# A Fourier filter with a gated convolution: other figures in the planner, seven subtractions on GpSimd, and a new order

## The chip, the cores and the metric

The kernel runs on one core of one Trainium2 chip. The time is device microseconds of that core, from the start of the program to its end; "before" is the median of three runs. The profile shows one further execution. Engines are named as the profile names them: PE (TensorE, matmuls; PEld its weight loads), DVE (VectorE), ACT (ScalarE), POOL (GpSimd), SP (SyncE, which issues most DMAs).

## The reference

Input x is 8 x 3200 x 256 in float32. A real Fourier transform runs along the 3200 positions, a complex 256 x 256 matrix mixes the channels, a bias is added, real and imaginary part are shrunk softly by 0.01, and the inverse transform goes back. The result passes a causal convolution of five taps per channel, a sigmoid, and a gate:

```
X = rfft(x, axis=1)
Yr = Xr @ w_r - Xi @ w_i + b_r ;  Yi = Xr @ w_i + Xi @ w_r + b_i
Y  = soft(Yr, 0.01) + 1j * soft(Yi, 0.01)        # sign(v) * max(|v| - lam, 0)
y  = irfft(Y, n=3200, axis=1)
gate = sigmoid(sum_k conv_w[k] * y[position - 4 + k])
out  = (gate * (y @ w_val)) @ w_out
```

## The kernel before

**Tiling.** The 3200 positions are 64 x 50. Each of the 8 batches goes through these stages; the names are those of the profile's rows (line numbers of the kernel before; behind line 350 the changed kernel's are one or two higher).

- P1 (L583; L549 for batch 0): the transform of length 50, in 8 parts of 400 KB of x. ACT copies the product to `s`, SP stores it to `a_dram`.
- 13 spectrum steps u, the last of half size. s2 (L634) multiplies `a`, read back from `a_dram`, by the twiddled matrix `f_sb`. ACT and DVE split the result into a high part (rounded) and a low part (the remainder), and do the same for the sum of its real and imaginary part (DVE L691, L692, L696). The complex mixing is done in three real products: the sum product (L709, into `k_bank`) and the mix (L704, into `y_ps`); for the half step it is L667 and L668. DVE adds the bias (L715; L670 for the half step) and the sum (L718), ACT and DVE shrink softly (L722, L724), and every second step the inverse product S1I (L747; L739 for the half step) goes through ACT to `z_dram`.
- 8 blocks of positions: `zl` is read back from `z_dram`, the inverse transform of length 50 (L803) gives `y_p`, ACT copies it to `y_sb`; behind the last block of a batch DVE copies the convolution's border (L816, L822).
- Gated convolution: ACT does the first tap (L857), DVE the other four (L860) on two blocks at a time, ACT the sigmoid (L871). y is split (ACT L360 high, DVE L362 remainder, tile `y_hl`), the v product (L835) follows, DVE multiplies the gate in (L902), the result is split in the same way (tile `gated`), the o product (L835) follows, ACT copies it to `o` (L926), SP stores it. For the last nine blocks (block 7 of batch 6 and all of batch 7, the list LATE_VAL) the v product works on unsplit y (L831, tile `w_late`, which POOL makes from the split weights, L937).

At the start matrix pieces are turned on PE (L469) for the inverse, and PE is kept busy with warm-up products on zeros (L951).

**What sets the order.** The program is first collected as pieces (function `add`: engine, duration, what it uses, what it sets, buffers). `Plan.order` then runs a list schedule over them with its own model: durations per engine (`dve`, `act`), DMA rates (RATE, PIPE), a fetch of the instructions of PE in packets (AHEAD, PACKET, TRIGGER, FETCH, QUEUE). Whenever several pieces could begin, the smallest due time `at` wins; due times are the step's place plus an offset from the table `O`. The engines run their queues in that order, so a changed figure can move any instruction. `WARM[2]` is the number of warm-up products ahead of the first s2. `split` makes a pair of high part and remainder. Pools set what can overlap: `ps_2` has two buffers, which P1, S1I, the positions, v and o all take in turn.

The seven blocks that the change's new flag picks are blocks 0 to 6 of batch 6: `LATE` lists the blocks of batches 6 and 7, and these seven are not in LATE_VAL.

## Time and profile before

| what | value |
|---|---|
| median of 3 runs | 879.93 us (878.89 to 881.42) |
| profiled execution | 881.59 us |
| its span, first to last instruction | 879.8 us |
| mean granted clock of PE | 0.994 |
| busy: PE, PEld, DVE, ACT, POOL | 857.8, 745.5, 759.1, 604.9, 3.8 us |
| bytes read from HBM and written to it | 82.05 and 79.69 MB |

A busy engine is one with an instruction in flight. Matmuls overlap, so the durations of their rows add up to more than the time they take; the distance from the start of one row to the next is what a product costs. An f32 matmul shows as two records, an fp32r one as one.

### The profile page before, as it was taken

Reading aid. Unit: us, or ns where it says so; the run is one execution under the profiler, and the core shown is the slowest. Engines: PE = TensorE matmul, PEld = TensorE weight load, DVE = VectorE, ACT = ScalarE, POOL = GpSimd, SP = SyncE. Lnnn points to the kernel's source line nnn. Section 1 sums busy time; section 2 is a strip of 40 time slices with the busy share of each in tenths; the row PEclk is TensorE's granted clock in tenths of the full one; section 3 lists DMA queues with packets and bytes.
Section 4 is the critical chain, followed back from the end, with each engine's and each line's share of the span. In section 5 each row is a group of like instructions: output and inputs, shape, how many; then the busy total and the mean of one; then the engine's idle time right before and its main releaser. Section 6 shows DMA issues by size and latency. Waiting matters only on the chain.

```text
span 879.8 us, 24544 instructions
## 1 busy us (share of the span) xinstructions
PE 857.8 (97%) x10400; PEld 745.5 (85%) x10400; DVE 759.1 (86%) x1143; ACT 604.9 (69%) x928; POOL 3.8 (0%) x11
## 2 busy tenths in 40 slices
PE   7999999999999999999999999999999999998997
PEld 3778788878999898898899889898899999998775
DVE  2346888999989996999879997899969999899796
ACT  2456666977677766877667776877658775875664
POOL 0000000000000000000000000000100000000000
PEclk9999999999999999999999999999999999999999
DMA  6878886786554476565855576646746353423522
GB/s 212 253 244 253 240 269 197 265 251 199 165 184 146 148 218 212 177 185 172 272 168 171 175 237 205 218 122 208 244 133 202 104 171 94 142 103 110 186 76 94
DMA packets 105289, 163.34 MB, mean 186 GB/s; under 512 B 9690, under 2 KB 78172, under 8 KB 105180
## 3 DMA queue, kind: packets, MB, share of 16 engines
q1 hardware_dynamic: 103764, 158.43, 58.1%
q10 hardware_dynamic: 1416, 3.34, 1.2%
q8 instruction: 82, 1.34, 0.6%
q14 instruction: 27, 0.22, 0.1%
HBM read 82.05 MB, written 79.69 MB: 184 GB/s over the span
## 4 chain that ended last, share of the span: by engine, by line
PE 78%; DVE 15%; DMA 3%; ACT 2%; issue 1%; SPq 0%; ACTq 0%; DVEq 0%
PE y_ps L704 14%; PE o_ps L835 12%; PE v_ps L835 11%; PE s L634 9%; PE z_ps L747 8%; PE k_bank L709 7%; PE y_p L803 6%; DVE acc L860 6%; PE p L583 5%; DMA x<-in_x 2%; PE warm L951 1%; DVE acc L902 1%; PE v_ps L831 1%; DMA f_sb<-in_f 1%; DVE gated L362 1%
## 5 line engine op out<-in xcount | busy, mean ns | idle before, releaser
L860 DVE SCALAR_TENSOR_TENSOR acc<-y_sb,cw_sb,acc 128x800 f32<-128x800 f32 (+1 forms) x264 | 258.7, 1017 | 11.4 <-ACT acc L857 11.2
L704 PE MATMUL y_ps<-w_sb,xs 128*128 128x256 f32 x1152 | 157.7, 286 | 0.7 <-DVE yb L718 0.7
L835 PE MATMUL o_ps<-gated,wo_sb 128*128 128x400 f32 x756 | 153.5, 352 | 0.0
L704 PEld LDWEIGHTS y_ps<-w_sb,xs 128*128 128x128 f32 x1152 | 144.3, 190 | 8.6 <-issue 3.9
L835 PEld LDWEIGHTS o_ps<-gated,wo_sb 128*128 128x128 f32 x756 | 135.6, 189 | 3.4 <-issue 1.0
L835 PE MATMUL v_ps<-y_hl,wv_sb 128*128 128x400 f32 x660 | 130.6, 346 | 1.1 <-ACT y_sb L810 1.1
L634 PEld LDWEIGHTS s<-f_sb,a 128*128 128x128 f32 x800 | 100.3, 191 | 24.9 <-issue 19.0
L835 PEld LDWEIGHTS v_ps<-y_hl,wv_sb 128*128 128x128 f32 x660 | 118.7, 188 | 2.1 <-ACT y_sb L810 1.3
L634 PE MATMUL s<-f_sb,a 128*128 128x128 f32 x800 | 111.9, 280 | 1.3 <-DVE xs L692 1.2
L747 PE MATMUL z_ps<-tp,g_sb 64*64 64x256 f32 x1536 | 93.7, 380 | 0.0
L688 ACT CAST xs<-s 128x512 fp32r<-128x512 f32 x96 | 56.2, 586 | 43.0 <-PE y_ps L704 28.1
L709 PE MATMUL k_bank<-w_sb,xs 128*128 128x256 f32 x576 | 85.3, 283 | 0.4 <-DVE yb L715 0.4
L722 ACT ACTIVATE tp<-yb,nlam 128x512 f32<-128x512 f32 (+1 forms) x104 | 73.6, 708 | 16.5 <-DVE yb L718 9.0
L718 DVE TENSOR_TENSOR yb<-y_ps,yb 128x512 f32<-128x512 f32 x96 | 65.4, 681 | 19.9 <-PE y_ps L704 19.7
L747 PEld LDWEIGHTS z_ps<-tp,g_sb 64*64 64x64 f32 x1536 | 57.1, 133 | 27.1 <-issue 5.8
L360 ACT CAST gated<-acc 128x800 fp32r<-128x800 f32 x63 | 54.2, 861 | 37.1 <-DVE acc L902 33.5
L709 PEld LDWEIGHTS k_bank<-w_sb,xs 128*128 128x128 f32 x576 | 74.8, 188 | 5.1 <-issue 1.1
L926 ACT COPY o<-o_ps 128x800 f32<-128x800 f32 x63 | 51.9, 823 | 38.0 <-PE o_ps L835 37.8
L803 PEld LDWEIGHTS y_p<-g_sb,zl 50*64 50x64 f32 x4096 | 66.1, 135 | 13.9 <-issue 5.1
L902 DVE TENSOR_TENSOR acc<-v_ps,acc 128x800 f32<-128x800 f32 x64 | 62.9, 983 | 16.9 <-PE v_ps L835 14.1
L724 DVE SCALAR_TENSOR_TENSOR tp<-yb,tp 128x512 f32<-128x512 f32 (+1 forms) x104 | 68.8, 661 | 7.7 <-ACT tp L722 7.4
L803 PE MATMUL y_p<-g_sb,zl 50*64 50x50 f32 x4096 | 71.8, 220 | 3.4 <-issue 2.2
(80 smaller groups left out, 1028.4 us busy)
## 6 DMA issues: line engine op xcount, KB each, us to landing
zl<-z_dram SPq DMA_DIRECT2D x128, 200.0 KB
out<-o SPq DMA_DIRECT2D x63, 400.0 KB
a_dram<-s SPq DMA_DIRECT2D x120, 208.0 KB
a<-a_dram SPq DMA_DIRECT2D x96, 256.0 KB
z_dram<-z_t SPq DMA_DIRECT2D x48, 512.0 KB
x<-in_x SPq DMA_DIRECT2D x120, 200.0 KB
...
```

Of the source, the lines that this page charges most:

```text
L634: nc.tensor.matmul(spec()[:, c, :, i, :], tl[ka][:, i0 + i, c * P:(c + 1) * P], f2_of(i), start=True, stop=True)
L688: nc.scalar.copy(out=tl[kx][:, 0:512], in_=tl[k2].rearrange("p a b -> p (a b)"))
L704: nc.tensor.matmul(p[:, 1 - r, :], xm(hx, c, r), w_sb[:, m, hw, c, :], start=k == 0, stop=k == 5)
L709: nc.tensor.matmul(p, sm(hx, c), w_sb[:, 0, hw, c, :], start=k == 0, stop=k == 5)
L718: add(at + 0.2, "DVE", dve(2 * D), lambda: nc.vector.tensor_tensor(out=yb(), in0=tl[ky], in1=yb(), op=ALU.add), [ky + (0,)], [kb + (0,)])
L722: nc.scalar.activation(out=buffer(kt, "tp", [P, 2, D])[:, 0:n], in_=tl[kb][:, 0:n], func=AF.Relu, bias=nlam)
L724: add(at + 0.2, "DVE", dve(n * D), lambda: nc.vector.scalar_tensor_tensor(out=tl[kt][:, 0:n], in0=tl[kb][:, 0:n], scalar=LAM, in1=tl[kt][: ...
L747: nc.tensor.matmul(p[e * HP:(e + 1) * HP, i, j * D:(j + 1) * D], g[i * HP:(i + 1) * HP, r, e * HP:(e + 1) * HP], tl[kts[j]][i * HP:(i + 1) ...
L803: nc.tensor.matmul(pv[h][e * HP:(e + 1) * HP, c, m, :], zt[half(h), m, c * P + e * HP:c * P + (e + 1) * HP], g2_sb[half(h), :], start=True ...
L835: nc.tensor.matmul(p[:, e, 0:TB], w[:, hw, c, e * P:(e + 1) * P], src(hy, c), start=n == 0, stop=n == 5)
L860: nc.vector.scalar_tensor_tensor(out=acc(c), in0=y_of(c, j), scalar=cw_sb[:, c, j:j + 1], in1=acc(c), op0=ALU.mult, op1=ALU.add)
L902: add(at + own("gate", b), "DVE", dve(2 * TB), lambda: nc.vector.tensor_tensor(out=gate(), in0=hn(tl[kv][:, :, 0:TB]), in1=gate(), op=ALU. ...
```

## The change

Figures of the planner:

```diff
-PIPE = {10: 235, 13: 300, 16: 324}
+PIPE = {10: 212, 13: 300, 16: 324}
-AHEAD, PACKET, TRIGGER, FETCH, QUEUE = 449, 256, 130, 5200, 0.6
+AHEAD, PACKET, TRIGGER, FETCH, QUEUE = 449, 256, 130, 7000, 0.6
-O = {'stay': -42.085,
+O = {'stay': 0.402,
...
-     's2': -2.447,
+     's2': -1.427,
...
-     'mix_sum': -0.971,
+     'mix_sum': -0.252,
...
-WARM = 4, 1, 19
+WARM = 4, 1, 10
+POOL_LOW = 2.7
```

PIPE and FETCH are the planner's own model: loads over ten DMA engines are taken as slower, the fetch of PE's instruction packets as longer. The table `O` is new in all its 35 entries. The remainder of y may go to GpSimd, and the last warm-up products are fewer and wider:

```diff
-    def split(at, n, key, src, high, low, uses=(), new=None, first=None):
+    def split(at, n, key, src, high, low, uses=(), new=None, first=None, pool=False):
...
-        add(at + 0.001, "DVE", dve(n), lambda: nc.vector.tensor_tensor(out=low(), in0=src(), in1=f32(high()), op=ALU.subtract),
+        eng, busy = ("POOL", POOL_LOW * n) if pool else ("DVE", dve(n))
+        add(at + 0.001, eng, busy, lambda: (nc.gpsimd if pool else nc.vector).tensor_tensor(out=low(), in0=src(), in1=f32(high()), op=ALU.subtract),
             [*uses, hl[0]], [hl[1]])
...
-                         lambda: buffer(ky, "y_hl", [P, 2, 2, TB], F32R)), ("w", "w_val", "high"), ("w", "w_val", "low")]
+                         lambda: buffer(ky, "y_hl", [P, 2, 2, TB], F32R), pool=bk in LATE), ("w", "w_val", "high"), ("w", "w_val", "low")]
...
-    def warm(n):
+    def warm(n, w=2 * P):
...
-            nc.tensor.matmul(pw.rearrange("p a b -> p (a b)")[:, 0:2 * P], tl[ki][:, 0:P], tl[ki][:, 0:2 * P], start=True, stop=True)
+            nc.tensor.matmul(pw.rearrange("p a b -> p (a b)")[:, 0:w], tl[ki][:, 0:P], tl[ki][:, 0:w], start=True, stop=True)
...
-        add(-22, "PE", 430, lambda: warm(1), [ki + (0,), ("turn", "p1", 7)], [kw + ("end", i)], ins=4)
+        add(-22, "PE", 860, lambda: warm(1, 4 * P), [ki + (0,), ("turn", "p1", 7)], [kw + ("end", i)], ins=4)
```

What it moves is shown at three places. First PE at the start, from the first sum product on (`k_bank<-w_sb` is the sum product, `k_bank<-eye_sb` a turning product, `s` is s2, `y_ps` the mix, `p` is P1). Before:

```order
L709 MATMUL k_bank<-w_sb,xs 128x256 x6
L583 MATMUL p_321<-x,f_sb 64x512 x4
L634 MATMUL s_308<-f_sb,a 128x2x64 x2
L583 MATMUL p_336<-x,f_sb 64x512 x4
L704 MATMUL y_ps<-w_sb,xs 128x256 x12
L583 MATMUL p_365<-x,f_sb 64x512 x4
L709 MATMUL k_bank<-w_sb,xs 128x256 x6
L634 MATMUL s_389<-f_sb,a 128x2x64 x2
L469 MATMUL k_bank<-eye_sb,f_sb 128x128 x2
L634 MATMUL s_389<-f_sb,a 128x2x64 x2
L469 MATMUL k_bank<-eye_sb,f_sb 128x128 x4
L704 MATMUL y_ps<-w_sb,xs 128x256 x12
```

Now:

```order
L711 MATMUL k_bank<-w_sb,xs 128x256 x6
L585 MATMUL p_312<-x,f_sb 64x512 x4
L706 MATMUL y_ps<-w_sb,xs 128x256 x12
L585 MATMUL p_341<-x,f_sb 64x512 x4
L585 MATMUL p_349<-x,f_sb 64x512 x4
L636 MATMUL s_299<-f_sb,a 128x2x64 x2
L711 MATMUL k_bank<-w_sb,xs 128x256 x6
L706 MATMUL y_ps<-w_sb,xs 128x256 x12
L471 MATMUL k_bank<-eye_sb,f_sb 128x128 x4
L636 MATMUL s_401<-f_sb,a 128x2x64 x2
L471 MATMUL k_bank<-eye_sb,f_sb 128x128 x4
L585 MATMUL p_415<-x,f_sb 64x512 x4
```

The second mix stands ahead of the turning products, which stood ahead of it, and the half s2 that stood ahead of the first of them now stands behind two.

Second, PE behind the half mix of the last batch, up to the position products (`y_p`) of that batch (`z_ps` is S1I, the single one of 128x256 the last). Before:

```order
L835 MATMUL o_ps<-gated,wo_sb 128x400 x12
L835 MATMUL v_ps<-y_hl,wv_sb 128x400 x12
L747 MATMUL z_ps<-tp,g_sb 64x256 x16
L739 MATMUL z_ps<-tp,g_sb 128x256
L835 MATMUL o_ps<-gated,wo_sb 128x400 x12
L835 MATMUL v_ps<-y_hl,wv_sb 128x400 x12
L835 MATMUL o_ps<-gated,wo_sb 128x400 x12
L835 MATMUL v_ps<-y_hl,wv_sb 128x400 x12
L831 MATMUL v_ps<-y_sb,w_late 128x400 x4
L803 MATMUL y_p<-g_sb,zl 64x50 x96
```

Now:

```order
L837 MATMUL v_ps<-y_hl,wv_sb 128x400 x12
L837 MATMUL o_ps<-gated,wo_sb 128x400 x12
L749 MATMUL z_ps<-tp,g_sb 64x256 x16
L837 MATMUL v_ps<-y_hl,wv_sb 128x400 x12
L837 MATMUL o_ps<-gated,wo_sb 128x400 x12
L741 MATMUL z_ps<-tp,g_sb 128x256
L837 MATMUL v_ps<-y_hl,wv_sb 128x400 x12
L837 MATMUL o_ps<-gated,wo_sb 128x400 x12
L837 MATMUL v_ps<-y_hl,wv_sb 128x400 x12
L833 MATMUL v_ps<-y_sb,w_late 128x400 x4
L837 MATMUL o_ps<-gated,wo_sb 128x400 x12
L805 MATMUL y_p<-g_sb,zl 64x50 x64
```

Four products of twelve matmuls stand ahead of the last S1I, and two did; one v product more stands behind the half mix than before.

Third, DVE over the same stretch, from the bias addition of the half mix on, with the numbers of the names, which rise in the order of issue over all engines (`acc<-y_sb` are taps, `acc<-v_ps` the gate products, `gated` and `y_hl` remainders). Before:

```order
L670 TENSOR_TENSOR yb_10340<-y_ps_10314,bias_sb_75 128x256
L362 TENSOR_TENSOR gated_10338<-acc_9963,gated_10338 128x800
L724 SCALAR_TENSOR_TENSOR tp_10349<-yb_10340,tp_10349 128x256
L860 SCALAR_TENSOR_TENSOR acc_10226<-y_sb_78,cw_sb_76,acc_10226 128x800 x4
L362 TENSOR_TENSOR y_hl_10327<-y_sb_78,y_hl_10327 128x800
L362 TENSOR_TENSOR y_hl_10391<-y_sb_78,y_hl_10391 128x800
L902 TENSOR_TENSOR acc_10226<-v_ps_10352,acc_10226 128x4x200
L860 SCALAR_TENSOR_TENSOR acc_10359<-y_sb_78,cw_sb_76,acc_10359 128x800 x2
L362 TENSOR_TENSOR gated_10403<-acc_10226,gated_10403 128x800
L860 SCALAR_TENSOR_TENSOR acc_10359<-y_sb_78,cw_sb_76,acc_10359 128x800 x3
L902 TENSOR_TENSOR acc_10226<-v_ps_10426,acc_10226 128x4x200
```

Now:

```order
L672 TENSOR_TENSOR yb_10320<-y_ps_10289,bias_sb_75 128x256
L862 SCALAR_TENSOR_TENSOR acc_10156<-y_sb_78,cw_sb_76,acc_10156 128x800
L904 TENSOR_TENSOR acc_9979<-v_ps_10306,acc_9979 128x4x200
L726 SCALAR_TENSOR_TENSOR tp_10323<-yb_10320,tp_10323 128x256
L862 SCALAR_TENSOR_TENSOR acc_10156<-y_sb_78,cw_sb_76,acc_10156 128x800
L364 TENSOR_TENSOR gated_10343<-acc_9979,gated_10343 128x800
L862 SCALAR_TENSOR_TENSOR acc_10156<-y_sb_78,cw_sb_76,acc_10156 128x800
L862 SCALAR_TENSOR_TENSOR acc_10369<-y_sb_78,cw_sb_76,acc_10369 128x800 x2
L904 TENSOR_TENSOR acc_10156<-v_ps_10371,acc_10156 128x4x200
L862 SCALAR_TENSOR_TENSOR acc_10369<-y_sb_78,cw_sb_76,acc_10369 128x800 x2
L364 TENSOR_TENSOR gated_10408<-acc_10156,gated_10408 128x800
```

And what stands on POOL now, where before only the first two of these rows stood:

```order
L939 TENSOR_TENSOR w_late_8708<-wv_sb_73 128x512
L939 TENSOR_TENSOR w_late_8708<-wo_sb_74 128x512
L364 TENSOR_TENSOR y_hl_9608<-y_sb_78,y_hl_9608 128x800
L364 TENSOR_TENSOR y_hl_9717<-y_sb_78,y_hl_9717 128x800
L364 TENSOR_TENSOR y_hl_9860<-y_sb_78,y_hl_9860 128x800
L364 TENSOR_TENSOR y_hl_10003<-y_sb_78,y_hl_10003 128x800
L364 TENSOR_TENSOR y_hl_10208<-y_sb_78,y_hl_10208 128x800
L364 TENSOR_TENSOR y_hl_10332<-y_sb_78,y_hl_10332 128x800
L364 TENSOR_TENSOR y_hl_10399<-y_sb_78,y_hl_10399 128x800
```

The remainders `y_hl` have left DVE's queue for POOL's, behind the making of `w_late`; taps and gate products have closed up.

More of the change, by code (lines that the diff above doesn't have):

```diff
@@ L256 @@
 T = float(NU)
-O = {'stay': -42.085,
-     'crowd': -50.453,
-     'hold': 7.335,
-     'together': 155.775,
-     'later': 18.484,
-     'load_x': 192.178,
-     'p1': -1.787,
-     'p1_step': 1.293,
-     'load_a': -41.005,
-     's2': -2.447,
-     's1i': 2.145,
-     'p3': 2.825,
-     'load_z': -29.254,
-     'y': 3.704,
-     'conv': 5.188,
-     'val': 5.514,
-     'gate': -19.992,
-     'project': 8.565,
-     'late_val': 7.079,
-     'late_out': 15.503,
-     'turn': -153.706,
-     'mix_sum': -0.971,
-     'p1_1': -89.715,
-     'load_x_1': 85.875,
-     'p1_2': 25.498,
-     'p3_6': -1.759,
-     'p3_7': -0.606,
-     'y_7': 18.885,
-     'conv_7': -29.176,
-     'val_7': 13.441,
-     'gate_7': -17.01,
-     'project_7': 13.598,
-     'p3_1': -0.93,
-     'p1_3': -6.723,
-     'p3_0': 0.056}
-WARM = 4, 1, 19
+O = {'stay': 0.402,
+     'crowd': -64.441,
+     'hold': -266.74,
+     'together': 101.712,
+     'later': 77.046,
+     'load_x': 139.522,
+     'p1': -4.034,
+     'p1_step': 1.65,
+     'load_a': -53.213,
+     's2': -1.427,
+     's1i': 3.004,
+     'p3': 2.236,
+     'load_z': -133.235,
+     'y': 22.146,
+     'conv': 21.172,
+     'val': 4.195,
+     'gate': -2.676,
+     'project': 6.28,
+     'late_val': 7.1,
+     'late_out': 15.6,
+     'turn': -209.166,
+     'mix_sum': -0.252,
+     'p1_1': -49.762,
+     'load_x_1': 189.6,
+     'p1_2': 34.586,
+     'p3_6': 1.163,
+     'p3_7': -1.565,
+     'y_7': 69.879,
+     'conv_7': -123.126,
+     'val_7': 54.086,
+     'gate_7': -98.61,
+     'project_7': 53.634,
+     'p3_1': -0.311,
+     'p1_3': -84.064,
+     'p3_0': -10.057}
+WARM = 4, 1, 10
 SLOTS = {"x": 3, "zl": 3, "y_hl": 2, "s1": 3, "a": 2, "xs": 2, "sx": 2, "xz": 1, "yb": 2, "tp": 3, "zst": 2,
          "acc": 2, "g_hl": 2, "o": 2, "ps_s2": 2, "ps_y": 1, "ps_k": 2, "ps_2": 2, "a_dram": 2, "z_dram": 2}
+POOL_LOW = 2.7
 LATE = [(b, k) for b in (B - 2, B - 1) for k in range(NB)]
```

## The prediction

> **What bounds the kernel now.** I read the page first: engines, slices, chain.
>
> ```profile
> span 879.8 us, 24544 instructions
> ...
> PE 857.8 (97%) x10400; PEld 745.5 (85%) x10400; DVE 759.1 (86%) x1143; ACT 604.9 (69%) x928; POOL 3.8 (0%) x11
> ...
> PE   7999999999999999999999999999999999998997
> ...
> DVE  2346888999989996999879997899969999899796
> ...
> PE 78%; DVE 15%; DMA 3%; ACT 2%; issue 1%; SPq 0%; ACTq 0%; DVEq 0%
> ```
>
> PE is busy 97% of the span and DVE 86%; by slices (22 us each) PE is full from the second to the thirty-sixth, DVE nearly so from the sixth on, and 78% of the chain that ended last is PE's, 15% DVE's. A busy PE need not be at its peak, so I looked at stretches next (us from the start; then the busy time of PE, PEld, DVE, ACT and POOL, the granted clock, the DMA share and GB/s).
>
> ```profile
> 40.00:60.00 20.00, 17.86 (x118) 12.37 (x122) 9.06 (x18) 9.77 (x19) 0.00 (x0) 0.91 0.83 240
> 560.00:600.00 40.00, 40.00 (x606) 36.45 (x605) 39.39 (x59) 32.31 (x50) 0.00 (x0) 1.00 0.61 187
> 700.00:720.00 20.00, 20.00 (x150) 19.54 (x143) 20.00 (x30) 15.35 (x25) 0.00 (x0) 1.00 0.45 133
> 780.00:800.00 20.00, 19.71 (x208) 18.23 (x210) 19.95 (x27) 15.73 (x22) 0.00 (x0) 1.00 0.26 93
> 800.00:820.00 20.00, 17.07 (x232) 14.70 (x226) 17.76 (x21) 10.22 (x14) 0.00 (x0) 0.91 0.46 155
> ```
>
> There are three parts. Up to about 60 us PE has holes that loads and copies leave. From there to about 780 PE is full; DVE is too wherever the gated convolution falls together with a spectrum step (20.00 of 20 at 700 to 720), but over 560 to 600 it still has some room. At 800 to 820 PE falls to 17.07 and the granted clock to 0.91. So a change in order can win only what PE waits at the start, at the end, and in small pieces between: counted from these rows 2.1 us at 40 to 60 and 2.9 at 800 to 820.
>
> The end, from the timeline (start, duration, engine, line; in brackets the idle time before and what ended it):
>
> ```profile
> 794.81 2.35 PE L835 MATMUL o_ps<-gated,wo_sb 128*128 128x400 f32 x12
> 795.83 0.41 DVE L670 TENSOR_TENSOR yb<-y_ps,bias_sb 128x256 f32<-128x256 f32 x1
> ...
> 797.39 3.93 DVE L860 SCALAR_TENSOR_TENSOR acc<-y_sb,cw_sb,acc 128x800 f32<-128x800 f32 x4
> ...
> 799.29 1.96 PE L747 MATMUL z_ps<-tp,g_sb 64*64 64x256 f32 x32
> ...
> 801.24 1.88 DVE L362 TENSOR_TENSOR y_hl<-y_sb,y_hl 128x800 fp32r<-128x800 f32 x2
> ...
> 804.17 1.19 PE L739 MATMUL z_ps<-tp,g_sb 128*128 128x256 f32 x2 [2.93 <-DVE acc L902]
> 804.80 3.63 PE L835 MATMUL o_ps<-gated,wo_sb 128*128 128x400 f32 x12
> ...
> 810.44 2.34 PE L835 MATMUL o_ps<-gated,wo_sb 128*128 128x400 f32 x12
> ...
> 812.62 2.33 PE L835 MATMUL v_ps<-y_hl,wv_sb 128*128 128x400 f32 x12
> ...
> 817.57 2.77 PE L803 MATMUL y_p<-g_sb,zl 50*64 50x50 f32 x157
> ...
> 819.64 0.37 DVE L816 COPY y_sb<-y_sb 128x400 f32<-128x400 f32 x1
> ...
> 821.35 0.78 PE L803 MATMUL y_p<-g_sb,zl 50*64 50x50 f32 x35 [1.02 <-issue]
> ...
> 823.90 7.79 DVE L860 SCALAR_TENSOR_TENSOR acc<-y_sb,cw_sb,acc 128x800 f32<-128x800 f32 x8 [3.55 <-ACT acc L857]
> ```
>
> The last mix (L667/L668, batch 7) ends where the o product of 794.81 begins; its bias addition on DVE (L670) starts 1.02 us later. S1Il, the last inverse product (L739), starts 9.36 us after the last mix and had PE idle for 2.93 us: the two-buffer pool `ps_2` had to be released by the gate product L902, which stood on DVE behind four taps (3.93) and two remainders (1.88 from 801.24). The product behind it took 3.63 us against 2.34 for the same form at 810.44; the granted clock of this stretch is the 0.91 shown above, and I put the 1.3 us down to that. From S1Il it is 13.40 us to the positions of the last batch (817.57), 2.07 more to the copy L816 on DVE (819.64), and 60.2 from there to the end of the span, in which DVE carries the taps.
>
> **The change, part by part.**
>
> *Start.* All rows up to the first sum product stand as they did. The warm-up's last part is 20 records of twice the width (10 products in two passes each) in place of 38:
>
> ```profile
> 30.76 4.05 PE L951 MATMUL warm<-idle 128*128 128x256 f32 x18
> ...
> 40.32 0.61 SPq L456 DMA_DIRECT2D f_sb<-in_f  x1
> ...
> 50.36 0.71 PE L469 MATMUL k_bank<-eye_sb,f_sb 128*128 128x128 f32 x4 [1.22 <-DMA f_sb<-in_f]
> ...
> 52.27 1.58 PE L469 MATMUL k_bank<-eye_sb,f_sb 128*128 128x128 f32 x8 [0.75 <-ACT g_sb L471]
> ...
> 53.50 2.90 PE L704 MATMUL y_ps<-w_sb,xs 128*128 128x256 f32 x12
> ```
>
> 18 records took 4.05 us, 0.225 each; 38 are 8.55 us, 20 at 0.45 are 9.0: +0.45. Then a turning product (L469) waited 1.22 us, until 50.36, for a part of `f_sb` asked for at 40.32, and the next, at 52.27, waited 0.75 for ACT's copy of its bank. The new order puts the second mix (here at 53.50) ahead of that turning product, in place of half an s2, while the load is issued at the same place of SP's queue: some 1.0 us more work stands in front of the wait. A gain of 1.22 + 0.75 at best, a loss of 0.45 and half a us more at worst if a P1 now waits for its x instead; I take -1.0 (ends -2.0 and +1.0), nearer to the printed wait for the load.
>
> *Order in the middle.* The same products run; only neighbours change. PE is full there, so what can be had is idle time that the waits show, for example of the position products, which come 64 or 96 in a row and wait for nothing that the profile shows:
>
> ```profile
> PE y_p L803 <- issue: 2.2, 5, 1.0
> ```
>
> 1.02 of this is the row of 821.35 after a run of 96. The new order breaks such runs at the end into 64, 32, 64 with o products between. I take -0.5 (ends -2.2, all of it, and +1.0, since shorter runs elsewhere come with new neighbours). The sum product now stands before the mix of its step, and the spectrum product s2 leads by one step, not two: between s2 and its sum product stand one sum, one mix and one s2, and no longer a second pair. That is the middle's risk; it is a rival below.
>
> *Last mix.* Behind the last mix 13 o and 4 v products of twelve matmuls stand now, 13 and 3 before. So one product less stands ahead of it, 812.62 - 810.44 = 2.18 us: the last mix ends 2.2 us earlier. Before S1Il there stand v, o, v, o (before: o, v), 4 x 2.18, and the S1I product (1.96 at most): 10.7 after the last mix in place of 9.36, but without the 2.93 us of idle time, if the gate product is there in time. From S1Il to the positions the same five products remain, 13.40 as it was, 12.1 if the clock stays at 1.00. With 2.07 to the copy L816 this path is 10.7 + 12.8 + 2.07 = 25.6 us (24.9 to 26.2) where it was 819.64 - 794.81 = 24.83: +0.8.
>
> *DVE's path over the same stretch.* Between L670 and the copy stood 22 instructions of the 128x800 kind, now 21 (the two remainders are gone; one more gate and one more remainder of `gated` are there, one tap fewer). Prices:
>
> ```profile
> L860 DVE SCALAR_TENSOR_TENSOR acc<-y_sb,cw_sb,acc 128x800 f32<-128x800 f32 x248 | 249.5, 1042 | 10.7 <-ACT acc L857 10.5
> L362 DVE TENSOR_TENSOR y_hl<-y_sb,y_hl 128x800 fp32r<-128x800 f32 x55 | 53.9, 982 | 2.8 <-ACT y_hl L360 2.5
> L696 DVE TENSOR_TENSOR xs<-sx,xs 128x256 fp32r<-128x256 f32 x96 | 40.4, 421 | 0.3 <-ACT xs L695 0.3
> L937 POOL TENSOR_TENSOR w_late<-wo_sb 128x512 f32<-128x512 f32 x1 | 1.5, 1463 | 0.0
> L937 POOL TENSOR_TENSOR w_late<-wv_sb 128x512 f32<-128x512 f32 x1 | 1.3, 1279 | 633.2 <-PE p L583 633.2
> ```
>
> 21 x 0.98 and 0.8 for the two short ones is 21.4, after the 1.02 of before: 22.4. That would leave PE's path, 25.6, as the longer one. Behind the copy DVE has one remainder of `gated` less: -1.0.
>
> *Seven remainders on GpSimd.* Off DVE: 7 x 0.982 = 6.9 us. On POOL, 128x512 of the same operation took 1279 and 1463 ns, 2.5 to 2.86 ns a column: 2.0 to 2.3 us for 800 columns, 2.15 taken. PE needs the results late enough: two v or o products, 4.4 us, stand in front even for the last one, so POOL's own length costs nothing. But the only place where POOL has worked beside DVE shows a price:
>
> ```profile
> 634.72 0.68 DVE L692 TENSOR_TENSOR xs<-s,xs 128x512 fp32r<-128x512 f32 x1
> 634.91 1.28 POOL L937 TENSOR_TENSOR w_late<-wv_sb 128x512 f32<-128x512 f32 x1 [633.18 <-PE p L583]
> 635.32 1.15 DVE L696 TENSOR_TENSOR xs<-sx,xs 128x256 fp32r<-128x256 f32 x1
> 636.13 1.46 POOL L937 TENSOR_TENSOR w_late<-wo_sb 128x512 f32<-128x512 f32 x1
> ```
>
> L696 reads two tiles in SBUF. Its mean is 421 ns; begun while POOL ran it took 1.15 us and ended 0.28 us after POOL's instruction. The L692 before it, which reads `s` in PSUM, took its usual 0.68. So I take it that such a DVE instruction stands still until POOL's is over. The taps (y_sb and acc), the remainders and L724 are of that kind, the gate product and the additions from PSUM are not. A hold costs between nothing (only PSUM readers in these 2.15 us) and 2.15 us. For the last three, which by the numbers in the names fall among taps, gate products and remainders of `gated`, I take 4.6 together, two of them full and a short one; for the first four, among more PSUM readers, 4.2, which the 3.9 us they save nearly pays back. DVE's path to the copy is then 22.4 + 4.6 = 27.0, longer than PE's 25.6: +2.2 against 24.83.
>
> [...]
>
> **The sum.** Start -1.0, middle -0.5, last mix earlier -2.2, stretch to the copy +2.2, behind the copy -1.0: -2.5 on a span of 879.8, 877.3. The profiled run took 881.59, 1.79 more than its span and 1.66 more than the median 879.93; against the median that is 877.4.
>
> **Rivals.**
> 1. *GpSimd and DVE run side by side.* Then PE's path decides the stretch, +0.8 in place of +2.2: 876.0. For it: a single row speaks for the hold. Against it: that row ends just behind POOL's.
> 2. *The hold decides (slower).* Every GpSimd remainder stops DVE for its 2.15 us: 15.0 for 6.9 saved. The last three make DVE's path 22.4 + 6.5 = 28.9, +4.1; the first four leave 4 x (2.15 - 0.98) = 4.7 of backlog, since DVE has no idle time at 700 to 720 and 0.05 of 20 at 780 to 800. -3.7 + 4.1 + 4.7 - 1.0 = +4.1: 884.0. It decides as soon as the holds on the last three pass 25.6 - 22.4 = 3.2 us.
> 3. *The shorter lead of s2 costs PE.* Against it: o or v products lie between most times. For it: no row of before shows so short a lead. If a third of the 96 steps (the count of L696) waits 0.15 us it is +4.8: 882.
> 4. *The new order gains its best ends,* -2.0 and -2.2 in place of -1.0 and -0.5: 874.7.
>
> **Chances.** My forecast 0.40, by its own terms 874.5 to 880.5; rival 1 0.22; rival 2 0.18; rival 3 0.12; rival 4 0.08. Three runs spread from 878.89 to 881.42, so 0.3% (2.6 us) is about what can be told from no change: below 877.3 is faster, above 882.5 slower. Half of my forecast lies below 877.3 and so does most of rivals 1 and 4: 0.43. Slower: rival 2 for the most part and some of 3: 0.21. The rest, 0.36, is no change. The range goes from 872.5 (a little under rival 4) to 884.5 (a little over rival 2).
>
> **What would show it.** In the changed profile: taps, `gated` remainders or L726 of over 2 us next to each of POOL's seven instructions, and POOL's seven at 2.0 to 2.5 us each (the hold); no idle time of 2 us ahead of the last inverse product, and the clock at 1.00 there (the released buffer); the first turning product without a wait of over 0.5 us (start); some 25.5 to 27 us from the last mix to the copy, and 59 from the copy to the end. The prediction is wrong if PE's waits in the middle grow by more than 3 us, if x or `f_sb` land later than before, or if DVE's holds fall where it has work for PE to wait for.

## The result: 1.5% slower, and the profile after

The changed kernel takes 894.22 us (median of four runs, 891.95 to 896.53) against 879.84 for the kernel before (four runs, the three of above among them, 878.89 to 881.42): ratio 1.0149, 95% interval 1.0121 to 1.0177. The forecast was 877.4, within 872.5 to 884.5. The profiled execution has a span of 892.9 us. Its page, engines, slices and chain:

```profile
span 892.9 us, 24521 instructions
...
PE 857.1 (96%) x10382; PEld 739.2 (83%) x10382; DVE 759.9 (85%) x1136; ACT 604.0 (68%) x928; POOL 18.4 (2%) x18
...
PE   7999998899999999999999999999989999998897
...
PE 64%; DVE 20%; DMA 7%; ACT 5%; issue 4%; SPq 0%; ACTq 0%; DVEq 0%
```

PE is busy for as long as before (857.1 against 857.8 us) in a span that is 13.1 us longer. So PE waits more, and the chain that ended last says the same: 64% PE where it was 78%; DVE's share rose from 15 to 20%, DMA's from 3 to 7%, ACT's from 2 to 5%, and time without a releaser ("issue") from 1 to 4%. The slices (22 us each) show where: eights in place of nines at the 7th, 8th, 30th and 38th.

The same by stretches, first before, then after (columns as in the prediction: PE, PEld, DVE, ACT, POOL busy, granted clock, DMA share, GB/s):

```profile
60.00:182.00 122.00, 119.65 (x1480) 98.43 (x1476) 101.07 (x194) 84.34 (x139) 0.00 (x0) 1.00 0.81 245
182.00:640.00 458.00, 457.26 (x5693) 408.40 (x5686) 423.05 (x621) 339.45 (x517) 2.69 (x2) 1.00 0.63 194
640.00:693.00 53.00, 52.57 (x819) 49.05 (x818) 46.04 (x69) 38.03 (x59) 0.00 (x0) 1.00 0.46 148
693.00:800.00 107.00, 106.52 (x1358) 99.96 (x1360) 103.59 (x149) 76.40 (x116) 0.00 (x0) 1.00 0.39 123
```

```profile
60.00:182.00 122.00, 114.66 (x1390) 93.34 (x1390) 98.86 (x192) 80.21 (x136) 0.00 (x0) 1.00 0.78 236
182.00:640.00 458.00, 453.50 (x5635) 407.03 (x5628) 420.59 (x613) 335.32 (x509) 0.00 (x0) 1.00 0.62 191
640.00:693.00 53.00, 50.18 (x769) 45.03 (x771) 43.51 (x64) 36.88 (x56) 2.98 (x2) 0.97 0.51 153
693.00:800.00 107.00, 105.79 (x1385) 99.19 (x1381) 101.44 (x149) 76.53 (x119) 9.88 (x5) 1.00 0.43 129
```

PE's idle time is the stretch less its busy time: 2.35, 0.74, 0.43, 0.48 before; 7.34, 4.50, 2.82, 1.21 after. From 60 to 693 us it grew by 11.1 us. POOL's seven remainders stand only in the last of these rows (five) and behind it (two); the two instructions at 640 to 693 make `w_late`, as the two at 182 to 640 did before. So most of the loss is there before GpSimd does any of its new work.

PE's longest entries in the list of waits (what waited, what ended it; total, times, longest):

```profile
PE s L636 <- issue: 3.2, 2, 2.8
PE y_p L805 <- issue: 2.6, 3, 1.4
PE y_p L805 <- DMA zl<-z_dram: 2.5, 3, 1.3
...
PE v_ps L837 <- ACT z_t L760: 2.1, 3, 1.7
PE k_bank L711 <- ACT xs L690: 1.7, 2, 1.0
PE p L585 <- ACT y_sb L812: 1.6, 1, 1.6
```

There are many small waits by many lines, where before one wait stood out (2.9 us at S1Il, which is gone). Two are singled out below: P1 that waits 1.64 us for ACT's copy of `y_sb`, and s2 that waits 2.82 us for nothing that the profile shows.

### The profile page after: what moved, and what is told of

It reads as the page before. It is cut to its first block, busy times and chain, and to the rows that moved or that the text cites. A ratio compares the mean times of both kernels' runs of the same rounds, so it can differ in the third digit from the quotient of the medians.

```text
span 892.9 us, 24521 instructions
## 1 busy us (share of the span) xinstructions
PE 857.1 (96%) x10382; PEld 739.2 (83%) x10382; DVE 759.9 (85%) x1136; ACT 604.0 (68%) x928; POOL 18.4 (2%) x18
## 4 chain that ended last, share of the span: by engine, by line
PE 64%; DVE 20%; DMA 7%; ACT 5%; issue 4%; SPq 0%; ACTq 0%; DVEq 0%
PE y_ps L706 12%; PE o_ps L837 11%; PE v_ps L837 9%; PE s L636 8%; DVE acc L862 8%; PE z_ps L749 6%; PE k_bank L711 6%; PE y_p L805 5%; PE p L585 4%; DVE acc L904 2%; PE v_ps L833 2%; DMA a_dram<-s 1%; DVE xs L694 1%; DVE yb L720 1%; DMA a<-a_dram 1%
## 5 line engine op out<-in xcount | busy, mean ns | idle before, releaser
L862 DVE SCALAR_TENSOR_TENSOR acc<-y_sb,cw_sb,acc 128x800 f32<-128x800 f32 (+1 forms) x264 | 266.4, 1033 | 13.1 <-ACT acc L859 12.7
L706 PE MATMUL y_ps<-w_sb,xs 128*128 128x256 f32 x1152 | 153.2, 282 | 0.1
L706 PEld LDWEIGHTS y_ps<-w_sb,xs 128*128 128x128 f32 x1152 | 142.5, 188 | 8.4 <-issue 3.2
L724 ACT ACTIVATE tp<-yb,nlam 128x512 f32<-128x512 f32 (+1 forms) x104 | 73.4, 706 | 40.2 <-DVE yb L720 25.5
L711 PE MATMUL k_bank<-w_sb,xs 128*128 128x256 f32 x576 | 89.8, 291 | 2.4 <-ACT xs L690 1.7
L805 PEld LDWEIGHTS y_p<-g_sb,zl 50*64 50x64 f32 x4096 | 67.9, 135 | 19.9 <-issue 4.6
L726 DVE SCALAR_TENSOR_TENSOR tp<-yb,tp 128x512 f32<-128x512 f32 (+1 forms) x104 | 70.6, 680 | 15.1 <-ACT tp L724 15.1
L711 PEld LDWEIGHTS k_bank<-w_sb,xs 128*128 128x128 f32 x576 | 75.8, 189 | 6.6 <-issue 2.4
L717 DVE TENSOR_TENSOR yb<-k_bank,bias_sb 128x512 f32<-128x512 f32 x96 | 65.5, 683 | 14.1 <-PE k_bank L711 8.9
L364 DVE TENSOR_TENSOR gated<-acc,gated 128x800 fp32r<-128x800 f32 x63 | 62.0, 984 | 7.5 <-ACT gated L361 7.4
```

The lines of the kernel that those rows point to most:

```text
L364: add(at + 0.001, eng, busy, lambda: (nc.gpsimd if pool else nc.vector).tensor_tensor(out=low(), in0=src(), in1=f32(high()), op=ALU.subtract),
L706: nc.tensor.matmul(p[:, 1 - r, :], xm(hx, c, r), w_sb[:, m, hw, c, :], start=k == 0, stop=k == 5)
L711: nc.tensor.matmul(p, sm(hx, c), w_sb[:, 0, hw, c, :], start=k == 0, stop=k == 5)
L717: nc.vector.tensor_tensor(out=buffer(kb, "yb", [P, 2, D]), in0=tl[kk].rearrange("p (a d) -> p a d", a=1).to_broadcast([P, 2, D]), in1=bias ...
L724: nc.scalar.activation(out=buffer(kt, "tp", [P, 2, D])[:, 0:n], in_=tl[kb][:, 0:n], func=AF.Relu, bias=nlam)
L726: add(at + 0.2, "DVE", dve(n * D), lambda: nc.vector.scalar_tensor_tensor(out=tl[kt][:, 0:n], in0=tl[kb][:, 0:n], scalar=LAM, in1=tl[kt][: ...
```

## The experiments

Many of the kernels run a given order, so that a stretch of an order, or GpSimd, can be looked at by itself. `ORDER` is the list of pieces as the planner of the kernel before put them out (the old order), as that of the changed kernel did (the new order), or as one did up to a cut and the other behind it (here and below, cuts of the code are shortened at "..."):

```diff
-            for p in self.order():
-                p["fn"]()
+            for n in ORDER:
+                self.pieces[n]["fn"]()
```

Below, "%" is the ratio to runs of the kernel before that were timed beside the run, less one; 0.1% is 0.88 us. Times in us are as measured. The intervals are some 0.2 to 0.3% to each side, so a difference between two kernels is good to some 2 to 4 us.

| run | what it is | time against before, 95% |
|---|---|---|
| pool_alone | old order, seven remainders on GpSimd | +0.32% (0.11 to 0.54) |
| pool_five | the same, five on GpSimd | -0.09% (-0.26 to 0.07) |
| pool_dummy | old order, GpSimd works beside, nothing saved | +0.59% (0.34 to 0.83) |
| order_alone | new order, remainders on DVE | +1.20% (0.91 to 1.48) |
| the change | new order, seven on GpSimd | +1.49% (1.21 to 1.77) |
| new_to_60 | new order to 60 us, then old | -0.09% (-0.28 to 0.10) |
| new_to_182 | new to 182 us, then old | +0.63% (0.38 to 0.87) |
| new_to_693 | new to 693 us, then old | +1.49% (1.20 to 1.77) |
| new_to_mix | new to the last mix, then old | +1.69% (1.42 to 1.95) |
| old_60_182 | new, but old from 60 to 182 us | +0.80% (0.49 to 1.10) |
| old_182_693 | new, but old from 182 to 693 us | +1.25% (1.05 to 1.45) |
| new_start_new_tail | old, but new to 60 us and behind the last mix | +0.29% (0.11 to 0.46) |
| spaced | new order, four products moved | +2.18% (1.87 to 2.48) |
| own_buffer | new order, one staging tile elsewhere | +0.97% (0.78 to 1.16) |
| clear_664 | new order, one position product moved | +1.26% (1.02 to 1.51) |
| old_O_new_figures | old table, PIPE 212 and FETCH 7000 | +1.32% (1.13 to 1.51) |
| new_O_old_figures | new table, PIPE 235 and FETCH 5200 | +1.97% (1.76 to 2.18) |
| fetch_5100 | old table, FETCH 5100 | -0.08% (-0.26 to 0.10) |
| fetch_5400 | old table, FETCH 5400 | +0.83% (0.68 to 0.99) |

All but the change, pool_alone and pool_five have all remainders on DVE.

### Order or GpSimd

`pool_alone` has the edit of `split` and its flag, in the old order on every engine; `order_alone` drops only the flag in the new one:

```diff
-                         lambda: buffer(ky, "y_hl", [P, 2, 2, TB], F32R), pool=bk in LATE), ("w", "w_val", "high"), ("w", "w_val", "low")]
+                         lambda: buffer(ky, "y_hl", [P, 2, 2, TB], F32R)), ("w", "w_val", "high"), ("w", "w_val", "low")]
```

> The order of the kernel before on every engine, old figures, old warm-up; only the seven remainders of batch 6 go to GpSimd, out of DVE's queue. Theory 1 (the loss sits in the new order of PE's products, the GpSimd part is small): 877.5 to 880.5, since 6.9 us leave DVE and the holds give some 5 back (in the changed kernel the lengthened DVE instructions add up to 5.2 us), and two of the seven stood ahead of the gate product that the last inverse product waits 2.93 us for. Theory 2 (the holds on DVE are the loss): 884, with each GpSimd remainder stopping DVE for 2 us or more.

> The changed kernel's order on every engine, its warm-up too; the seven remainders stand on DVE, each where it stood in the issue order. Theory 1 (order): 892 to 897, the loss stays, and DVE takes 6.9 us more work less 5.2 us of holds. Theory 2 (holds): 880 to 886, the loss goes with GpSimd.

Measured: 883.11 us (+0.32%) and 891.76 us (+1.20%). The order carries 1.20 of the 1.49%. GpSimd costs 0.32% (2.8 us) in the old order; in the new one it is 1.49 - 1.20 = 0.29%, which lies within the intervals of the two runs. Theory 1 is right on the order, but its 877.5 to 880.5 for GpSimd was too low: taking 6.9 us off DVE made the kernel slower. Where that comes from, in `pool_alone` (timeline):

```profile
757.24 11.38 DVE L860 SCALAR_TENSOR_TENSOR acc<-y_sb,cw_sb,acc 128x800 f32<-128x800 f32 x8 [1.19 <-ACT acc L857]
...
760.52 2.71 POOL L362 TENSOR_TENSOR y_hl<-y_sb,y_hl 128x800 fp32r<-128x800 f32 x1 [5.57 <-ACT y_hl L360]
...
764.26 2.54 POOL L362 TENSOR_TENSOR y_hl<-y_sb,y_hl 128x800 fp32r<-128x800 f32 x1 [1.03 <-ACT y_hl L360]
...
767.69 1.83 ACT L871 ACTIVATE acc<-acc 128x800 f32<-128x800 f32 x2 [2.78 <-DVE acc L860]
...
770.61 2.44 PE L835 MATMUL v_ps<-y_hl,wv_sb 128*128 128x400 f32 x12 [0.77 <-DVE acc L902]
```

Eight taps take 11.38 us. Behind them wait the sigmoid (ACT idle for 2.78), the gate product and PE. Before, the two remainders that GpSimd does here stood on DVE behind these taps, and the sigmoid followed the taps without a wait.

### The holds by themselves

`pool_five` leaves those two on DVE. `pool_dummy` saves nothing: each of the seven remainders stays on DVE, and GpSimd subtracts 768 columns of the same tiles into `b_sb`, which nobody reads any more:

```diff
# pool_five
-    pool=bk in LATE)
+    pool=bk in LATE and k not in (1, 2))
# pool_dummy
-    lambda: (nc.gpsimd if pool else nc.vector).tensor_tensor(out=low(), in0=src(), in1=f32(high()), op=ALU.subtract)
+    lambda: (nc.vector.tensor_tensor(out=low(), in0=src(), in1=f32(high()), op=ALU.subtract),
+             pool and nc.gpsimd.tensor_tensor(out=b_sb..., in0=src()[:, :, :, 0:192], in1=f32(high())[:, :, :, 0:192], op=ALU.subtract))
```

> As the run with GpSimd alone (old order), but the remainders of blocks 1 and 2 of batch 6 stay on DVE; the other five are on GpSimd. In that run the eight taps beside those two GpSimd instructions took 11.38 us in place of some 7.9, and behind them stood the sigmoid, the gate product and two waits of PE (0.77 and 0.53 us). Theory 1 (holds cost where DVE's chain is late, elsewhere nothing): 879.5 to 881, the 2.5 us of loss gone, since two remainders of 0.98 stand behind the taps again. Theory 2 (the loss is GpSimd's own longer latency, 2 us against 1, before the v products): 882.5 to 883.5, since the last five have it too.

> The kernel before with nothing taken off DVE: next to each of the seven remainders of batch 6 GpSimd makes a further subtraction of 128x768 from the same tiles into a tile that nobody reads any more. Theory 1 (GpSimd stops a DVE instruction with two SBUF inputs until its own is over): DVE's taps and remainders beside the seven get 4 to 8 us longer together, and the time is 883 to 888, more than with GpSimd doing the remainders (883.1), as nothing is saved. Theory 2 (side by side, and the loss with GpSimd alone came from its latency): 880 to 881, no longer DVE instructions.

Measured: -0.09% and +0.59%: theory 1 both times. A longer way of GpSimd's results to PE is not the cause in `pool_dummy`, as nobody waits for them. The eight taps, first in `pool_five`, then in `pool_dummy`:

```profile
755.84 8.04 DVE L860 SCALAR_TENSOR_TENSOR acc<-y_sb,cw_sb,acc 128x800 f32<-128x800 f32 x8 [1.19 <-ACT acc L857]
```

```profile
757.63 11.30 DVE L860 SCALAR_TENSOR_TENSOR acc<-y_sb,cw_sb,acc 128x800 f32<-128x800 f32 x8 [1.19 <-ACT acc L857]
...
760.79 1.85 POOL L362 TENSOR_TENSOR b_sb<-y_sb,y_hl 128x768 f32<-128x768 f32 x1 [4.72 <-ACT y_hl L360]
...
764.54 2.58 POOL L362 TENSOR_TENSOR b_sb<-y_sb,y_hl 128x768 f32<-128x768 f32 x1 [1.90 <-ACT y_hl L360]
...
797.88 1.85 POOL L362 TENSOR_TENSOR b_sb<-y_sb,y_hl 128x768 f32<-128x768 f32 x1 [7.46 <-ACT y_hl L360]
...
798.15 2.43 DVE L860 SCALAR_TENSOR_TENSOR acc<-y_sb,cw_sb,acc 128x800 f32<-128x800 f32 x1
...
805.28 4.20 POOL L362 TENSOR_TENSOR b_sb<-y_sb,y_hl 128x768 f32<-128x768 f32 x1 [5.55 <-ACT y_hl L360]
...
805.92 1.88 DVE L362 TENSOR_TENSOR y_hl<-y_sb,y_hl 128x800 fp32r<-128x800 f32 x2
```

The taps take 8.04 us without GpSimd beside them, and 11.30 and 11.38 with two instructions of it, whether or not anybody reads what those compute. The rows show a hold in both directions. The instruction of 797.88 takes 1.85 us, and the tap that begins 0.27 us behind it takes 2.43 in place of 1.04. That of 764.54 begins while a tap is under way and takes 2.58; that of 805.28 begins during a tap, two remainders follow on DVE, and it takes 4.20.

### Where the order loses

Four runs begin with the new order and go on with the old one from a cut on; three have the old order in a piece between. At 60 and 182 us and ahead of the last mix both orders have issued the same PE products; at 693 us all but some 3 us of them.

> The changed kernel's order and warm-up up to its 60 us, from there the order of the kernel before; all remainders on DVE. At the cut both orders have issued the same PE products. Up to there the changed kernel's PE has waited 3.4 us less. Theory 1 (a wait of PE counts in full wherever it stands, as PE is the bound): 876.4, the 3.4 us stay. Theory 2 (what is gained at the start is waited for again behind it, by loads and copies that have not moved): 879 to 880.

> The changed kernel's order and warm-up up to its 182.4 us, from there the order of the kernel before; all remainders on DVE. At the cut both orders have issued the same PE products. Between 60 and 182 us the changed kernel's PE has waited 6.2 us more. Theory 1 (these waits belong to the new order of batches 0 and 1 and count in full): 882.6. Theory 2 (they are made up for behind, the old order having slack): 878 to 880. Against new_to_60 theory 1 gives 6.2 us, theory 2 under 2.

> The changed kernel's order up to its 693 us (behind the stall of 2.9 us at 664 us), from there the order of the kernel before; all remainders on DVE. Up to there the changed kernel's PE has waited 9.9 us more than the kernel before, 2.8 of them by 182 us and 7.1 between 182 and 693, half of those in the one wait at 664. Theory 1 (waits of PE inside the order add up): 885.7 of the run cut at 182 + 7.1 = 892.8, so that nearly all of the loss is there before the tail. Theory 2 (the loss behind 182 us comes from the tail, the last 200 us): 886 to 888.

> The changed kernel's order up to its last mix (801.7 us), from there the order of the kernel before; all remainders on DVE. At the cut both orders have issued the same PE products. Theory 1 (the tail's order is worse, in the changed kernel with the remainders on DVE by less than with GpSimd): 889 to 891, 1 to 3 us under the changed order with remainders on DVE (891.8). Theory 2 (the tail's order is better, since the wait of 2.93 us ahead of the last inverse product stands in the old tail alone): 893 to 895.

> The changed kernel's order up to 60 us, the order of the kernel before over the products that the changed kernel runs between 60 and 182 us, then the changed order again; all remainders on DVE. At both cuts the two orders have issued the same PE products. This is the other half of the runs cut at 60 and at 182 us, which gave 5.8 us for this piece. Theory 1 (the order of these 120 us costs what its waits add up to): 885.5 to 886.5, 5.8 us under the changed order with remainders on DVE (891.8). Theory 2 (the loss lies in how loads and batches behind are placed, which this piece only shifts): 890 to 892.

> The changed order, but the order of the kernel before from 182 us to 693 us (at 182 both have issued the same PE products, at 693 all but some 3 us of the same); all remainders on DVE. The cuts at 182 and at 693 gave 6 us for this piece. Theory 1 (the order there costs it): 885 to 887, some 6 us under 891.8. Theory 2 (carried over, or bound to how the piece begins): 890 to 892.

> The changed order up to 60 us, the order of the kernel before from there to the last mix, the changed order from the last mix on (it has one v product more to run there); all remainders on DVE. Theory 1 (gains and losses sit in the stretches and add up: start -0.7, the tail behind the last mix -3 to -4 by the runs so far): 875 to 877, faster than both kernels. Theory 2 (the new tail is only good behind the new middle, whose last v product it takes over and whose DVE arrives differently): 879 to 882.

Measured: -0.09, +0.63, +1.49, +1.69, +0.80, +1.25 and +0.29%. The start is worth 0.8 us (2.5 to -0.9), not the 3.4 us by which PE waited less in the profiled run. That run had no spell of half clock in its first 60 us (mean granted clock 1.00), and the profiled run of before had two (0.94 over the same 60 us).

A piece can be weighed in two ways: by what it adds to the old order, and by what taking it out of the new order saves. From 60 to 182 us it adds 0.63 + 0.09 = 0.72% and saves 1.20 - 0.80 = 0.40%; from 182 to 693 it adds 0.86 and saves -0.05; the tail adds 0.29 + 0.09 = 0.38 and saves -(1.69 - 1.20) = -0.49. Each time adding costs more than taking out saves, by more than the intervals for the last two. So a cut seems to have a price of its own; that loads and copies are placed for one order would explain it, and was not tested. The mean of the two ways is 0.56%, 0.41% and -0.05%: some 5 us for 60 to 182, 3.6 for 182 to 693, nothing for the tail's order, each good to a few us and no better than the two ways agree. What is left of the 1.20% is 0.3 to 0.4% between 693 us and the last mix, within the intervals. Theory 1 (waits simply add up) was the nearer one for the cuts at 182 and 693 us (882.6 and 892.8 expected, 885.68 and 893.64 measured). For the cuts at 60 us and at the last mix it was theory 2; old_60_182 lies between the two (888.66). Theory 1 failed for old_182_693 and for the tail: new_start_new_tail, expected to beat both kernels, is slower than the kernel before. No run here beats the kernel before by more than its interval.

### One wait traced to its cause

Between 60 and 182 us PE has two waits of over 1.1 us, 1.64 at 137.74 and 1.68 at 176.78. The first, from the timeline of the changed kernel (PE, DVE and ACT):

```profile
133.21 1.15 PE L805 MATMUL y_p<-g_sb,zl 50*64 50x50 f32 x64
...
134.43 0.43 DVE L403 TENSOR_SCALAR st<-st 128x512 int32<-128x512 int32 x1 [3.15 <-PE y_p L805]
...
136.56 0.40 ACT L697 CAST xs<-sx 128x256 fp32r<-128x256 f32 x1 [3.77 <-DVE sx L693]
136.87 0.82 ACT L812 COPY y_sb<-y_p 128x800 f32<-128x800 f32 x1
...
137.74 1.09 PE L585 MATMUL p<-x,f_sb 50*64 50x512 f32 x8 [1.64 <-ACT y_sb L812]
```

Read from below: P1 waits for ACT's copy of the position product; that copy stands behind L697, for which ACT waited 3.77 us; L697 needs a sum that stood on DVE behind L403, and L403 waited 3.15 us for the position product of 133.21. L403 is a step in the conversion of `w_out`. Its third staging tile comes from the pool of `zl`, which has three buffers. The new order puts the first load of `zl` between the first staging tile and the other two, so four tiles share three buffers, and the last has to wait until the position product has read `zl`. The same shortage stops SyncE, which issues the loads in order: its next load of `zl` waits for the conversion to give a buffer back (from the changed kernel's list of waits):

```profile
SPq L790 <- DVE st L403: 8.7, 1, 8.7
```

In the old order that load stands behind the conversion. The planner lets this through: for a piece that opens two tiles of one pool, `opens` looks at the same old buffer twice.

`own_buffer` puts that one tile in a pool not yet in use. `spaced` leaves the buffers as they are and sets four waiting products apart by s2, sum or mix products; on SyncE one load of x and one store change places with it.

```diff
# own_buffer
-        keys = [("st%d" % j, name) for j in range(3)]
+        keys, OTHER = [("st%d" % j, name) for j in range(3)], "g_hl" if name == "w_out" else "zl"
...
-   {k: "zl" for k in keys[1:]}
+   {keys[1]: "zl", keys[2]: OTHER}
# spaced: ORDER with P1 of 137.7 behind the next sum, the s2 of 146.97 ahead of the positions of 145.1,
#         the sum of 174.1 ahead of the P1 of 173.1, the next mix ahead of the v of 176.8
```

> The changed order with the remainders on DVE; the third staging tile of w_out's conversion (st2) lies in a buffer of the pool of gated, which is not used yet, in place of the third zl buffer. In the changed order the load of zl for the first positions stands between w_out's staging tiles, so that four tiles share three buffers, and DVE stands still for 3.15 us at 131.3 us until the position product has read zl. Theory 1 (this wait is passed on: DVE's splits late, ACT's copies late, P1 waits 1.64 us): DVE's wait and PE's 1.64 are gone, 889 to 890.5 against 891.8. Theory 2 (PE's wait there has another cause): PE's wait stays, 891.8.

> The changed kernel's order with the remainders on DVE; between 130 and 180 us four of the products that take one of the two ps_2 buffers are set apart by s2, sum or mix products that followed them (P1 at 137.7, positions at 145.1, P1 at 173.1, v at 176.8 us of the changed kernel). The waits ahead of these four are 1.64, 0.36 + 0.46, 0.88 and 1.68, 5.0 us together. Theory 1 (they are the turn-around of the two buffers, and distance fills them): 887 to 888.5, and the waits there under 1.5 us together. Theory 2 (ACT or DVE is behind there, and the wait only moves to the next product): 891 to 892.

`own_buffer`: 1.0097 against 1.0120, 2 us less in the runs, which the intervals (1.0078 to 1.0116 and 1.0091 to 1.0148) allow but do not force. In the trace the chain is gone: the same step on DVE, and the same P1, stand without a bracket, and SyncE's wait of 8.7 us is gone too:

```profile
131.46 0.41 DVE L403 TENSOR_SCALAR st<-st 128x512 int32<-128x512 int32 x1
...
136.19 1.04 PE L585 MATMUL p<-x,f_sb 50*64 50x512 f32 x8
```

From matmul 900 (123 us) to matmul 1300 (154 us) this kernel makes up 3.7 us against `order_alone`. So this cause is shown for PE's waits from 131 to 154 us; the waits of 0.88 and 1.68 us at 173 and 177 stay in it.

`spaced` speaks against both theories: +2.18%. The P1 of 149.56 waits for its x (timeline of `spaced`):

```profile
149.56 1.08 PE L585 MATMUL p<-x,f_sb 50*64 50x512 f32 x4 [1.95 <-DMA x<-in_x]
151.02 2.80 PE L585 MATMUL p<-x,f_sb 50*64 50x512 f32 x12 [0.38 <-DMA x<-in_x]
153.75 1.65 PE L711 MATMUL k_bank<-w_sb,xs 128*128 128x256 f32 x6
```

That load is issued at 143.59, in `order_alone` at 141.95: on SyncE it stands behind the load of `zl` that waits for L403 (until 142.3 here, 141.2 there), and now also behind the store, since the moved P1 reads the buffer that it takes. From 151.9 to 158.7 us the clock is granted at half (0.50 over 155 to 158 us), so that a sum takes 1.65 us in place of 0.95. Over the same matmuls this kernel lost 5 us against `order_alone`. The waits did not come from the distance between products: I had taken the last link of the chain for its cause.

### The wait that nothing ended

At 664 us (timeline of the changed kernel):

```profile
663.15 1.10 PE L805 MATMUL y_p<-g_sb,zl 50*64 50x50 f32 x64
664.18 0.71 PE L636 MATMUL s<-f_sb,a 128*128 128x128 f32 x4
667.71 1.01 PE L636 MATMUL s<-f_sb,a 128*128 128x128 f32 x4 [2.82 <-issue]
```

s2 stops half way, and no semaphore ends it. In the DMA records packets of 16 KB on the queue of instructions start at 656.7 and 665.1 us. Between them 190 matmuls begin, 128 of them in two position products of 64 that take 1.1 us each, and the DMA engines are 83% busy. `clear_664` moves the position product of 663.15 behind the s2 and v products that follow; with it the next mix and o product change places, and on SyncE a load of `zl` and a store.

> The changed kernel's order with the remainders on DVE; one position product (64 matmuls, at 662.9 us in the changed kernel) moved behind the s2 and the v product that followed it. Theory 1 (PE runs out of instructions at 664 us: 64-matmul products use them up faster than packets of instructions come, behind loads of zl): the wait without a releaser falls from 2.6 to 2.9 us to under 1, and the time from 891.8 to 888.5 to 889.5. Theory 2 (that s2 waits for something else that the profile does not show): the wait stays ahead of that s2, 891.8.

The wait is gone from the trace; the s2 product runs in one piece:

```profile
662.36 1.16 PE L636 MATMUL s<-f_sb,a 128*128 128x128 f32 x8
```

The time is +1.26%, no better than `order_alone` (which had the wait, 2.57 us): part came back as waits behind (0.47 us for ACT's copy of `o` at 672 us), and what is left is below what the runs tell. That PE ran out of instructions is what the traces point to; it is not shown. `fetch_5400` and `new_O_old_figures`, below, have such a wait of 2.54 us each, at 264 us in a position product and at 262 us in a v product, and in all three a packet of instructions ends during the wait and PE goes on 1.35 to 1.71 us after its end (1.51 here). The run shows that the wait goes with the order of these products; what holds the packets up was not tried.

### What drew the new order

> The kernel before with the two figures of the planner alone (PIPE 212, FETCH 7000), planned anew: table O, warm-up and remainders as before. Theory 1 (the table O carries the loss, the figures move neighbours and little else): 878 to 883. Theory 2 (the figures make the bad order, since a longer fetch and slower loads in the model push products apart from where they fit): 886 to 893.

> The changed table O and warm-up with the old figures (PIPE 235, FETCH 5200), planned anew, remainders on DVE. Theory 1 (the table): 888 to 895, near the changed order with the remainders on DVE (891.8). Theory 2 (the figures): 879 to 885.

Both 1.3 and 2.0% slower: the new figures with the old table lose about as much as the whole change, and the new table with the old figures loses more. Neither theory holds. With the new figures the two tables are equal within the intervals (+1.32 and +1.20%); the new table is 0.8% worse with the old figures than with its own. Planned with PIPE 212 alone, the kernel before has the same order on every engine, so it is FETCH that redraws. The last two runs move only that figure, by 2 and 4%:

```diff
-AHEAD, PACKET, TRIGGER, FETCH, QUEUE = 449, 256, 130, 5200, 0.6
+AHEAD, PACKET, TRIGGER, FETCH, QUEUE = 449, 256, 130, 5100, 0.6
```

> The kernel before with FETCH 5100 in place of 5200 and nothing else, planned anew. Theory 1 (the order before is a picked one, and any redrawn one loses about as much as the change did): 886 to 893. Theory 2 (it is the value 7000 that makes the order bad): 879 to 882.

> The kernel before with FETCH 5400 in place of 5200 and nothing else, planned anew. Theory 1 (any redrawn order loses): 886 to 893. Theory 2 (the value 7000): 879 to 883, between the kernel before and nothing.

-0.08% and +0.83%. Neither theory holds for both: a redrawn order need not lose, and a step of 4% can cost 7 us. Besides the 2.9 us at S1Il, which the kernel before has too, the two longest waits of `fetch_5400` between 60 and 880 us are a mix at 164 us (2.5), whose bank DVE reads late, and the position product at 264 us that nothing releases (2.5):

```profile
PE y_p L803 <- issue: 5.3, 8, 2.5
PE z_ps L739 <- DVE acc L902: 2.9, 1, 2.9
PE y_ps L704 <- DVE yb L718: 2.9, 2, 2.5
```

So the change set two figures that by themselves make the planner's order no better, and a table that gives another order out of many: of five redrawn ones timed here, one equals the kernel before and four are 0.8 to 2.0% slower. The planner's own end time, which `Plan.order` works out from each kernel's file, is 864.2 us for the kernel before, 864.5 with FETCH 5100, 871.5 with 5400 and 885.5 with 7000, though a longer fetch is itself part of that. It puts these three in the measured order (-0.08, +0.83, +1.32%). For the changed kernel it gives 866.1 us, 0.2% more, where 1.5% was measured, so most of what the new order loses is not in that model. Whether the order before is a rare good one, no run here tells.

## Why the prediction was wrong

The failed step is *Order in the middle*, -0.5 us with ends of -2.2 and +1.0. PE's idle time grew by 11.1 us from 60 to 693 us, and the cuts put some 8.5 us there (0.56 + 0.41%; 13.9 us by what it adds to the old order, 3.1 by what taking it out saves). In its place stand waits that the new order makes: one is traced to a buffer of the pool of `zl` (1.64 us and what follows it), one to 664 us (2.82, cause open), and the many small ones are not traced. The gain was bounded by rows: PE had only so much idle time to lose. The loss was not: +1.0 stood on no row. The rows of before showed the waits that the old order has, which bounds what a new order can win, and nothing about the waits that a new order makes. The list of what would make the prediction wrong named it (waits in the middle by over 3 us), but the sum gave it no room.

By the steps:

- *Start, -1.0.* The run cut at 60 us gives -0.8 (-2.5 to 0.9). Right as far as it can be told; the turning product that had waited 1.22 us for `f_sb` waits 0.7 now.
- *Rival 3, the shorter lead of s2, 882.* Right in sign, wrong in mechanism and far too low. The tenth percentile of the time from the last split to its sum product went from 1.79 to 0.75 us, but only six of the 96 sum products start within 0.3 us of it, and the waits of this kind are the 1.7 us of L711 above.
- *Last mix 2.2 us earlier.* The last mix ends at 803.17, 8.4 us later than before, although it has one product less ahead of it. That is the start and the middle.
- *Last mix to the copy, 27.0 us.* It took 28.6 (after's timeline):

```profile
803.17 2.36 PE L837 MATMUL v_ps<-y_hl,wv_sb 128*128 128x400 f32 x12
...
814.90 0.60 PE L741 MATMUL z_ps<-tp,g_sb 128*128 128x256 f32 x2
816.48 2.46 PE L837 MATMUL v_ps<-y_hl,wv_sb 128*128 128x400 f32 x12 [0.98 <-ACT o L928]
...
822.09 2.46 PE L837 MATMUL v_ps<-y_hl,wv_sb 128*128 128x400 f32 x12 [0.74 <-DVE acc L904]
...
829.34 1.15 PE L805 MATMUL y_p<-g_sb,zl 50*64 50x50 f32 x64
...
831.79 0.37 DVE L818 COPY y_sb<-y_sb 128x400 f32<-128x400 f32 x1 [0.46 <-ACT y_sb L812]
```

  The last inverse product L741 starts without the 2.93 us of before, and at full clock (1.00 over 814 to 816 us), as forecast. But it starts 11.73 us after the last mix (10.7 forecast), the positions 14.44 behind it (12.8) and the copy 2.45 behind those (2.07). The released wait came back in pieces of 0.6 to 1 us. `order_alone` takes 27.2 us for the same stretch, so 1.5 of the 28.6 came with GpSimd in these two traces.
- *Holds, 8.8 us together against 6.9 saved.* That GpSimd stops such DVE instructions is right; the size is too high. POOL's seven took 1.91 to 2.43 us (2.0 to 2.5 forecast). Rows of the changed kernel:

```profile
761.29 3.08 DVE L862 SCALAR_TENSOR_TENSOR acc<-y_sb,cw_sb,acc 128x800 f32<-128x800 f32 x2
...
783.03 2.17 DVE L862 SCALAR_TENSOR_TENSOR acc<-y_sb,cw_sb,acc 128x800 f32<-128x800 f32 x1
...
807.02 1.78 DVE L726 SCALAR_TENSOR_TENSOR tp<-yb,tp 128x256 f32<-128x256 f32 x1
...
814.66 3.65 DVE L862 SCALAR_TENSOR_TENSOR acc<-y_sb,cw_sb,acc 128x800 f32<-128x800 f32 x2
```

  Two taps take 2.00 us undisturbed, one 1.04, L726 of this form 0.42. That is 1.08 + 1.13 + 1.36 + 1.65, with two small ones (0.12 and 0.16) 5.5 us: 2.3 for the first four (4.2 forecast) and 3.2 for the last three (4.6). Less was held than saved, and still GpSimd did not pay: in the old order, with 5.1 us held (3.3 of them in the eight taps), it cost 0.32%. The step that failed here is to set held against saved time: in `pool_alone` nothing had waited for the two remainders behind the eight taps, and the holds hit taps with the sigmoid, the gate product and PE behind them. `pool_five`, which takes those two holds away, loses nothing. Rival 2 had its loss of 4 us from the same sum.
- *Behind the copy, -1.0.* It took 61.1 us from the copy to the end, 60.2 before: +0.9, and 62.8 in `order_alone`, so this is the order's and not GpSimd's.

The range missed because its upper end, 884.5, was rival 2's, and rival 2 had no waits of a new order in it. Nothing on the page bounded those, so the upper end should have lain far higher; the five redrawn orders here reach 2.0%.
